# Attention and routed experts on one core: scores by half blocks in quarters of the array, probabilities turned by products with the unit matrix

## The chip, the cores and the metric

The kernel runs on one core of a Trainium2 chip. The metric is the device time in microseconds of one execution; 753.51 us is the median of three runs before the change.

## What is computed

The attention part works on 4 batches with 8 heads, 768 positions and 64 columns per head. Each query sees the 4 first keys (the sinks) and a window of 128 keys that ends with its own; its result is the row of the expert part, 3072 rows of 512 columns. Each row then goes to two of 8 experts (512 to 1024 to 512, with a rectifier between).

```python
keep = is_sink | in_window            # pos < 4, or 0 <= rel < 128
scores = np.where(keep, scale * q @ k.T, -1e9)
a = np.exp(scores - scores.max(-1)); a = a / (a.sum(-1) + 1e-9)
attn_out = a @ v
# experts
noisy = x @ w_gate + np.log1p(np.exp(x @ w_noise)) * noise
top2, top2_w = two largest of noisy, softmax over the two
out[mask] += top2_w[mask, k, None] * (np.maximum(x[mask] @ w1[e], 0) @ w2[e])
```

## The kernel before, in words

The program has two phases. The first is the attention of all batches, with the routing of a batch woven in behind it; the second is the experts. A batch has 4 pairs of heads; a pair, g, has its two heads in the two halves of the partitions. Each pair takes 3 steps, so there are 48 steps n, and a step works on two blocks of 128 queries for two heads, four units in all.

For a step, `qk` (L389) makes the scores of one block at a time, twice per step: a stationary tile of 128 queries against the block before and the block itself, 2 x 132 columns (4 of them sinks). The two heads use the upper and the lower half of the array's rows. Each of the two calls takes a buffer of two banks, S. `prev` (L392, ScalarE) moves the scores of the older block and the sinks, 132 columns for each unit, into `cbuf`; `cur` (L399, VectorE) puts the newer block's scores over those of the older block where the key is not later than the query. By that a unit keeps 132 columns, since exactly one of the keys j and j + 128 is in the window. In the first block of a pair `cur` is an addition of a mask (L397). `mins` (L409, VectorE) takes the maximum, `minus_max` (L412, GpSimd) negates it, `exps_sums` (L423, ScalarE) makes the exponentials with their sums.

`ptr` (L465, L468) turns the probabilities by transposes on TensorE into a buffer P of two banks; on odd steps also the sink columns that `pcopy` (L458, GpSimd) has laid together for two steps. `ptr_c` (L474, ScalarE) moves the turned tile to CT; `ptr_m` (L484, GpSimd's affine select) makes CM, the same with the older block's part set to zero. `pv` multiplies CT with the values of the older block (L494) and CM with `dv`, the difference of the two blocks' values (L497; the difference is L300, on GpSimd for two pairs in four, else on VectorE). `sinks` (L509) adds the sinks' part, `pv_c` (L517, ScalarE) moves the result, `rows` (L523, VectorE) turns it for the store. L436 (GpSimd) and L450 (VectorE) make the reciprocals of the sums.

S, P and the logits' buffer A share three double banks (`HELD = dict(D=3, X=2)`); X, the result of `pv`, has two single banks. Values and differences have two buffers each (`vn=2, dv=2`), so the values of a pair can be loaded when the pair two before it is done.

Every operation of the first phase is registered with its engine, and the order in which they are issued is the list `ORDER`, a list of operation numbers written out by hand; each engine then runs its instructions in that order, the SP queue its loads and stores as well. `replay` also gives each S, P, A and X its bank, by the time at which a planner expects a bank to be free. On SP, four writes of the routing weights (L848, `keep`) and the loads of keys (L364) and values (L367) stand in one queue. In the routing, L822 and L828 count rows by products with a matrix of ones, and the results of a batch give the first rows of expert 0.

The second phase is a list of matrix products, L1157 to L1159 (up, three products with split weights and rows) and L1223 to L1225 (down), ordered by the planner.

## Time and profile before

| | |
|---|---|
| median of 3 runs | 753.51 us (750.51 to 756.1) |
| profiled execution | 756.2 us, of which its span 754.6 us |
| mean granted clock of TensorE | 0.988 |
| busy in the span | PE 729.2, PEld 618.4, DVE 418.1, ACT 339.5, POOL 393.6 us |
| instructions | 13413 |

PE is TensorE's products, PEld its weight loads, DVE is VectorE, ACT ScalarE, POOL GpSimd. The times of two executions differ by some tenths of a per cent, so the profiled one is compared with its own span and not with the median.

### The profile page before, as it was taken

To read this page: it belongs to the slowest core of one execution; us is meant where nothing else is said; L and a number is where in the kernel's file an instruction comes from. 1 tells how busy PE (TensorE), PEld (TensorE's weight loads), DVE (VectorE), ACT (ScalarE), POOL (GpSimd) and SP (SyncE) were. 2 spreads that over 40 slices of the span, in tenths; PEclk is the share of its full clock that TensorE was granted. 3 is DMA by queue.
4 is the path that set the end of the run, shared out by engine and by line. 5 is a ranking of instruction groups with operands and counts; after the bars stand their busy time and mean duration, and the time that the engine had idled before them with its cause. 6 is when DMAs were issued, how large, how long until landed. Compare 5 with 4: busy or idle time off the path is not lost.

```text
span 754.6 us, 13413 instructions
## 1 busy us (share of the span) xinstructions
PE 729.2 (97%) x4787; PEld 618.4 (82%) x4787; DVE 418.1 (55%) x1082; ACT 339.5 (45%) x907; POOL 393.6 (52%) x640
## 2 busy tenths in 40 slices
PE   8999899889999999999999999999999999999995
PEld 4766666567889898889889988998899999999994
DVE  5779688786754654654365446535652664473420
ACT  5999799785224413341333243323432441343221
POOL 4346458771237385456636573747284755647212
PEclk9999899989999999999999999999999999999998
DMA  6557687945546743553445354526351653454033
GB/s 227 194 174 221 147 260 170 266 89 153 155 145 145 241 100 60 152 144 63 87 141 132 51 98 144 123 50 154 128 101 28 157 165 62 83 172 74 15 43 43
DMA packets 58310, 97.30 MB, mean 129 GB/s; under 512 B 19296, under 2 KB 31840, under 8 KB 58240
## 3 DMA queue, kind: packets, MB, share of 16 engines
q1 hardware_dynamic: 44864, 68.82, 30.3%
q0 software_dynamic: 13376, 27.60, 20.5%
q8 instruction: 38, 0.62, 0.4%
q14 instruction: 32, 0.26, 0.1%
HBM read 67.99 MB, written 28.40 MB: 128 GB/s over the span
## 4 chain that ended last, share of the span: by engine, by line
PE 77%; ACT 8%; issue 4%; DMA 4%; DVE 3%; POOL 2%; POOLq 0%; ACTq 0%; SPq 0%; DVEq 0%
PE H L1159 11%; PE H L1157 11%; PE H L1158 11%; PE Y L1224 11%; PE Y L1225 11%; PE Y L1223 11%; ACT cbuf L423 4%; PE D L389 3%; PE X L494 1%; ACT cbuf L392 1%; ACT CT L474 1%; PE Y L1228 1%; PE Y L1229 1%; POOL out L1247 1%; PE X L350 1%
## 5 line engine op out<-in xcount | busy, mean ns | idle before, releaser
L1008 POOL DMA_INDIRECT xg<-x_rows,rt_idq x174 | 174.2, 1001 | 60.9 <-issue 51.3
L1204 ACT ACTIVATE h<-H 128x384 fp32r<-128x384 f32 (+4 forms) x127 | 63.8, 503 | 254.5 <-PE H L1159 254.3
L1158 PE MATMUL H<-sqn,w 128*128 128x384 f32 (+4 forms) x508 | 174.0, 343 | 0.9 <-DVE sqn L300 0.9
L1157 PE MATMUL H<-skn,w 128*128 128x384 f32 (+4 forms) x508 | 174.5, 344 | 0.0
L1159 PE MATMUL H<-skn,w 128*128 128x384 f32 (+4 forms) x508 | 174.3, 343 | 0.0
L1212 DVE SCALAR_TENSOR_TENSOR h<-H,h 128x384 fp32r<-128x384 f32 (+4 forms) x167 | 75.1, 470 | 163.7 <-ACT h L1204 163.2
L1247 POOL DMA_INDIRECT out<-y,idx x53 | 93.7, 1767 | 50.5 <-ACT y L1232 34.9
L1256 POOL COPY spacer<-h 1x1 f32<-1x1 f32 x88 | 28.0, 319 | 147.4 <-ACT h L1204 147.2
L1158 PEld LDWEIGHTS H<-sqn,w 128*128 128x128 f32 x508 | 95.4, 188 | 7.7 <-DVE sqn L300 1.2
L1157 PEld LDWEIGHTS H<-skn,w 128*128 128x128 f32 x508 | 95.4, 188 | 7.4 <-ACT skn L1075 0.4
L1159 PEld LDWEIGHTS H<-skn,w 128*128 128x128 f32 x508 | 95.3, 188 | 2.1
L423 ACT ACTIVATE cbuf<-cbuf,nb 128x132 f32<-128x132 f32 x192 | 75.6, 412 | 2.4 <-POOL nb L412 2.4
L1225 PE MATMUL Y<-w2a,h 128*128 128x512 f32 x192 | 75.6, 394 | 0.0
L1225 PE MATMUL Y<-w2b,h 128*128 128x512 f32 x192 | 75.6, 394 | 0.0
L1224 PE MATMUL Y<-w2a,h 128*128 128x512 f32 x192 | 75.5, 393 | 0.0
L1224 PE MATMUL Y<-w2b,h 128*128 128x512 f32 x192 | 75.5, 393 | 0.0
L1223 PE MATMUL Y<-w2b,h 128*128 128x512 f32 x192 | 75.1, 391 | 0.0
L1223 PE MATMUL Y<-w2a,h 128*128 128x512 f32 x192 | 74.8, 389 | 0.0
L389 PE MATMUL D<-kq 64*128 64x264 f32 (+1 forms) x384 | 57.1, 406 | 9.2 <-DVE cbuf L399 3.6
L1075 ACT ACTIVATE skn<-xtn 128x512 fp32r<-128x512 f32 (+2 forms) x46 | 27.8, 605 | 58.5 <-DVE xtn L1066 58.4
L389 PEld LDWEIGHTS D<-kq 64*128 64x128 f32 x384 | 31.6, 192 | 21.1 <-DVE cbuf L399 6.0
L399 DVE COPY_PREDICATED cbuf<-le,D 128x256 f32<-128x256 uint8 x80 | 34.7, 445 | 18.4 <-ACT cbuf L392 17.8
(210 smaller groups left out, 1203.8 us busy)
## 6 DMA issues: line engine op xcount, KB each, us to landing
st<-in_w1l SPq DMA_DIRECT2D x32, 512.0 KB, 4.4
st<-in_w2l SPq DMA_DIRECT2D x32, 512.0 KB, 4.1
kq<-in_kq SPq DMA_DIRECT2D x15, 792.0 KB, 6.5
out<-zt SPq DMA_DIRECT2D x31, 256.0 KB, 5.6
vn<-in_v SPq DMA_DIRECT2D x16, 384.0 KB, 5.8
x_rows<-xr SPq DMA_DIRECT2D x48, 128.0 KB, 5.0
xg<-x_rows,rt_idq POOLq DMA_INDIRECT x174, 2.8
out<-y,idx POOLq DMA_INDIRECT x53, 5.1
```

Of the source, the lines that this page charges most:

```text
L389: nc.tensor.matmul(p[:, :2 if j else 1], kq(g)[r, j // 2, 2 + j % 2, NS:], x[:, :2 if j else 1], start=True, stop=True)
L423: nc.scalar.activation(C(n)[:, u], C(n)[:, u], AF.Exp, bias=get("nb", n)[:, u:u + 1], scale=1.0 / math.sqrt(D), accum_out=get("sm", n // 2 ...
L1008: nc.gpsimd.indirect_dma_start(out=x[:, i, :], out_offset=None, in_=xbuf.rearrange("r (q d) -> (r q) d", d=sh.SW), in_offset=bass.Indirect ...
L1157: nc.tensor.matmul(p, w[:, 0], xh, start=(i == 0), stop=False)
L1158: nc.tensor.matmul(p, w[:, 0], xl, start=False, stop=False)
L1159: nc.tensor.matmul(p, w[:, 1], xh, start=False, stop=(i == sh.DM // 128 - 1))
L1204: nc.scalar.activation(get("h", FC * q + f, [128, 2 * 128 * FIRST], F32R)[:, :width], H(q, f), AF.Relu)
L1212: nc.vector.scalar_tensor_tensor(h[:, o:o + s1 - s0], p[:, s0:s1], 0.0, h[:, s0:s1].bitcast(F32), op0=OP.max, op1=OP.subtract)
L1223: nc.tensor.matmul(p, hh, w[:, 0], start=(f == 0), stop=False)
L1224: nc.tensor.matmul(p, hh, w[:, 1], start=False, stop=False)
L1225: nc.tensor.matmul(p, hl, w[:, 0], start=False, stop=(f == FC - 1))
L1247: d = nc.gpsimd.indirect_dma_start(out=out, out_offset=bass.IndirectOffsetOnAxis(ap=c["idx"][:size(e, t), e, t:t + 1], axis=0), in_=get("y ...
```

## The change: what it does

The layout of the keys and queries in memory becomes one row of 6 blocks of 132 columns (128 keys and the 4 sinks) for the keys, and one for the queries. `qk` is called once per step. Each block of 128 queries is cut into two halves of 64; a half sees 196 columns in one piece, 128 keys from the start of its window, the sinks between, and 64 more. A product has 64 rows (a head) and 64 columns of queries (a half), so the four products of a block take the four quarters of the array. The four units of a step lie in one buffer of two banks. `prev` moves the first 132 columns of all units in one instruction, on ScalarE or VectorE; `cur` puts the last 64 columns over the first 64 in one instruction. In the first block of a pair, `cur0` adds a mask to the 132 columns before that, and `nosink` falls away.

`ptr` makes 16 products of 64 x 64 with the unit matrix in place of 8 transposes of 64 x 128 (20 in place of 10 on odd steps); `pcopy` takes two instructions, since the sinks lie in other columns in the two halves.

Some operations can now stand on another engine, as the string `SIDE` says for each: of 48 moves `prev`, 11 go to VectorE (6 of these on ordinary steps, 5 on first ones); of the 24 moves `ptr_c` of even steps, 7; of the 48 `pv_c`, 15; 11 of 48 `minus_max`, 7 of 24 `sums_e` and 3 of 16 `cur1` go from GpSimd to VectorE; 15 of 24 `pcopy` go from GpSimd to ScalarE. All 16 differences `dv` are on GpSimd, and a third of the `ptr_m` (16 of 48) on VectorE, where they read P. The order is another one, and `BANKS` names the banks.

```diff
@@ -18,7 +18,7 @@
-PR = dict(load_qk=0.0, load_v=24.264, w1=36, pc_pool=0, gap_8=1, dv_pool=2, et=42, cm_pool=12, gap=4, subs=0)
+PR = dict(load_qk=0.0, load_v=24.264, w1=36, pc_pool=0, gap_8=1, dv_pool=4, et=42, cm_pool=8, gap=4, subs=0)
@@ -38,54 +38,57 @@
 ORDER = """
...
+0 1 8 72 2 4 73 9 10 12 6 14 11 16 118 18 13 20 74 22 15 3 24 26 17 28 30 173 19 32 5 34 76 221 21 36 38 120 23 40
...
+"""
+SIDE = """
+11000011101001010001000100100000001000000011001000000100000100010100010000110000110000000100010000010000000010001111
+00010010111000001011010000011000101100100100010010100010100000001000010000100100000100010001011101011001000001001000
+"""
+BANKS = """
+00120120110120012001120101200112001012001012012001011001012102101020121102021120211102100121010021102011100210112112
+0110210020011001121002201201210102002010210100112012
@@ -124,10 +128,15 @@
-    def op(self, eng, dur, prio, fn, r=(), w=(), u=(), lat=None, kind=0):
+    def op(self, eng, dur, prio, fn, r=(), w=(), u=(), lat=None, kind=0, alt=None):
+        if alt:
+            self.alts.append((i, (eng, dur, kind), alt))
+            if SIDE.replace("\n", "")[len(self.alts) - 1:len(self.alts)] == "1":
+                eng, dur, kind = alt
+            fn.__defaults__ = fn.__defaults__[:-1] + (eng,)
@@ -240,12 +249,13 @@
-                    x = self.slot[kx] = len(r) - 1 if kx in last else min(range(len(r)), key=lambda x: r[x])
+                    x = self.slot[kx] = int(banks[len(self.slot)]) if banks else len(r) - 1 if kx in last else min(
+                        range(len(r)), key=lambda x: r[x])
@@ -303,13 +313,17 @@
-    m0 = consts.tile([128, 128], F32, name="m0")
-    nc.vector.tensor_scalar(m0, jp, 0.0, -BIG, op0=OP.is_gt, op1=OP.mult)
+    half = slice(0, 64), slice(64, 128)
+    m0 = consts.tile([128, KW], F32, name="m0")
+    nc.vector.memset(m0, -BIG)
+    for r, o, x in ((half[0], 0, jp[:, :128]), (half[1], 0, jp[:, 64:128]), (half[1], 64 + NS, jp[:, :64])):
+        nc.vector.tensor_scalar(m0[r, o:o + x.shape[1]], x[r], 0.0, -BIG, op0=OP.is_gt, op1=OP.mult)
-    nc.vector.tensor_copy(m1, m0[:, :NS])
-    nc.vector.memset(m0[:, :NS], 0.0)
-    le = consts.tile([128, 128], U8, name="le")
-    nc.vector.tensor_scalar(le, jp, 0.0, None, op0=OP.is_le)
+    nc.vector.tensor_scalar(m1, jp[:, :NS], 0.0, -BIG, op0=OP.is_gt, op1=OP.mult)
+    nc.vector.memset(m0[half[0], :NS], 0.0)
+    le = consts.tile([128, 64], U8, name="le")
+    for r in half:
+        nc.vector.tensor_scalar(le[r], jp[r, r], 0.0, None, op0=OP.is_le)
@@ -333,7 +347,7 @@
-    KW = 128 + NS
+    KW, BW = 128 + NS, 192 + NS
@@ -371,45 +385,58 @@
-    def keys(g, j0):
-        t = kq(g).rearrange("p g x k -> p (g x) k")
-        f = j0 // 2 * 4 + j0 % 2
-        return t[:, f:f + 2] if j0 % 2 == 0 else t[:, f:f + 4:3]
-
-    def qk(n, a):
-        g, j, _ = at(n, 2 * a)
-        for h in range(2):
-            r = slice(h * D, (h + 1) * D)
-            p = get("S", 2 * n + a, [128, 2, 512], F32, "ps")[:, h, :2 * KW].rearrange("p (a b) -> p a b", a=2)
-            x = keys(g, max(j - 1, 0))[r]
-            nc.tensor.matmul(p[:, :2 if j else 1], kq(g)[r, j // 2, 2 + j % 2, NS:], x[:, :2 if j else 1], start=True, stop=True)
-
-    def prev(n, a):
-        nc.scalar.activation(C(n)[:, 2 * a:2 * a + 2, :], get("S", 2 * n + a)[:, :, :KW], AF.Copy)
-
-    def cur(n, a):
-        c, p = C(n)[:, 2 * a:2 * a + 2, NS:], get("S", 2 * n + a)
-        if at(n, 2 * a)[1] == 0:
-            nc.vector.tensor_tensor(c, p[:, :, NS:KW], m0[:, None, :].to_broadcast([128, 2, 128]), op=OP.add)
+    def scores(n):
+        return get("S", n, [128, 2, 512], F32, "ps")[:, :, :2 * BW].rearrange("p h (a k) -> p a h k", a=2)
+
+    def qk(n):
+        for a in range(2):
+            g, j, _ = at(n, 2 * a)
+            for i in range(2):
+                for h in range(2):
+                    r, t = slice(h * D, (h + 1) * D), slice(64 * i, 64 * i + 64)
+                    k, x = kq(g)[r, 0].rearrange("p b k -> p (b k)"), scores(n)[t, a, h]
+                    k0 = KW * (j - 1) + 64 * i
+                    for o, f, w in ((0, k0, BW),) if j else ((0, 64 * i, KW - 64 * i), (64 + NS, 0, 64))[:1 + i]:
+                        nc.tensor.matmul(x[:, o:o + w], kq(g)[r, 1, j, t], k[:, f:f + w], start=True, stop=True)
+
+    def moved(eng, out, x):
+        if eng == "DVE":
+            nc.vector.tensor_copy(out, x)
-            nc.vector.copy_predicated(c, le[:, None, :].to_broadcast([128, 2, 128]), p[:, :, KW + NS:2 * KW])
-
-    def nosink(n):
-        nc.gpsimd.memset(C(n)[:, :2, :NS], -BIG)
-
-    def cur1(n):
-        c = C(n)[:, 2:, NS:2 * NS]
-        nc.gpsimd.tensor_tensor(c, c, m1[:, None, :].to_broadcast([128, 2, NS]), op=OP.add)
+            nc.scalar.activation(out, x, AF.Copy)
+
+    def small(eng):
+        return nc.gpsimd if eng == "Pool" else nc.vector
+
+    def old(n):
+        return int(n % NJ == 0)
+
+    def units(n):
+        return C(n).rearrange("p (a h) k -> p a h k", a=2)
+
+    def prev(n, eng):
+        moved(eng, units(n)[:, old(n):], scores(n)[:, old(n):, :, :KW])
+
+    def cur0(n):
+        nc.vector.tensor_tensor(units(n)[:, 0], scores(n)[:, 0, :, :KW], m0[:, None, :].to_broadcast([128, 2, KW]), op=OP.add)
+
+    def cur(n):
+        c = units(n)[:, old(n):, :, :64]
+        nc.vector.copy_predicated(c, le[:, None, None, :].to_broadcast([128, 2 - old(n), 2, 64]), scores(n)[:, old(n):, :, KW:])
+
+    def cur1(n, eng):
+        c = C(n)[:, 2:, :NS]
+        small(eng).tensor_tensor(c, c, m1[:, None, :].to_broadcast([128, 2, NS]), op=OP.add)
-    def minus_max(n):
-        nc.gpsimd.tensor_scalar(get("nb", n, [128, 4]), get("mn", n), -1.0 / math.sqrt(D), None, op0=OP.mult)
+    def minus_max(n, eng):
+        small(eng).tensor_scalar(get("nb", n, [128, 4]), get("mn", n), -1.0 / math.sqrt(D), None, op0=OP.mult)
@@ -432,8 +459,8 @@
-    def sums_e(m):
-        nc.gpsimd.tensor_scalar(get("sm", m), get("sm", m), 1e-9, None, op0=OP.add)
+    def sums_e(m, eng):
+        small(eng).tensor_scalar(get("sm", m), get("sm", m), 1e-9, None, op0=OP.add)
@@ -450,28 +477,30 @@
-        t = pcbuf[:, m % plan.rings["pc"]].rearrange("p (g x u s) -> p g x u s", g=2, x=4, u=4)[:, :, 0]
-        c = cbuf[:, 2 * (m % (plan.rings["C"] // 2)):][:, :2, :, :NS]
-        if eng == "ACT":
-            nc.scalar.activation(t, c, AF.Copy)
-        else:
-            (nc.gpsimd if eng == "Pool" else nc.vector).tensor_copy(t, c)
+        for i in range(2):
+            r, k = slice(64 * i, 64 * i + 64), 64 if i else 128
+            t = pcbuf[r, m % plan.rings["pc"]].rearrange("p (g x u s) -> p g x u s", g=2, x=4, u=4)[:, :, 0]
+            c = cbuf[r, 2 * (m % (plan.rings["C"] // 2)):][:, :2, :, k:k + NS]
+            if eng == "ACT":
+                nc.scalar.activation(t, c, AF.Copy)
+            else:
+                (nc.gpsimd if eng == "Pool" else nc.vector).tensor_copy(t, c)
-        for u in range(4):
-            for i in range(2):
-                r = slice(64 * i, 64 * i + 64)
-                nc.tensor.transpose(p[:, i, 64 * u:64 * u + 64], C(n)[r, u, NS:], idf[r, r])
-        for i in range(2 if n % 2 else 0):
-            r = slice(64 * i, 64 * i + 64)
-            nc.tensor.transpose(p[:, i, 256:320], pcbuf[r, n // 2 % plan.rings["pc"], :], idf[r, r])
+        for u in range(5 if n % 2 else 4):
+            for t in range(2):
+                for i in range(2):
+                    r = slice(64 * i, 64 * i + 64)
+                    x = C(n)[r, u] if u < 4 else pcbuf[r, n // 2 % plan.rings["pc"], :]
+                    k = (68 - 68 * t if i else 64 * t) if u < 4 else 64 * t
+                    nc.tensor.matmul(p[64 * t:64 * t + 64, i, 64 * u:64 * u + 64], x[:, k:k + 64], idf[r, r], start=True, stop=True)
-    def ptr_c(n):
-        nc.scalar.activation(get("CT", n, [128, 4, 128]).rearrange("p u (i s) -> p u i s", i=2), turned(n), AF.Copy)
+    def ptr_c(n, eng=0):
+        moved(eng, get("CT", n, [128, 4, 128]).rearrange("p u (i s) -> p u i s", i=2), turned(n))
@@ -513,8 +542,8 @@
-    def pv_c(n):
-        nc.scalar.activation(xt(n), get("X", XA[n])[:, :2, :], AF.Copy)
+    def pv_c(n, eng):
+        moved(eng, xt(n), get("X", XA[n])[:, :2, :])
@@ -563,24 +592,22 @@
+            need = {jj, max(jj - 1, 0)}
+            op("PE", .68 if jj else .61, n + P(g, "qk"), lambda n=n: qk(n), r=[("kq", g, i) for i in need], w=[("S", n)],
+               u=[("kq", g), ("C", n)], kind=3)
+            op("ACT", .46 if jj else .27, n + P(g, "prev"), lambda n=n, e=0: prev(n, e), r=[("S", n)], w=[("C", n, 0)], u=[("C", n)],
+               alt=("DVE", .61 if jj else .34, 0))
-                op("Pool", .05, n + P(g, "nosink"), lambda n=n: nosink(n), w=[("C", n, 0)], u=[("C", n)])
-            for a in range(2):
-                z = n + .2 * a
-                s = 2 * n + a
-                need = [jj] if not jj or a else [jj - 1, jj]
-                op("PE", .45 if jj or a else .26, z + P(g, "qk"), lambda n=n, a=a: qk(n, a),
-                   r=[("kq", g, i) for i in {jj, *need}], w=[("S", s)], u=[("kq", g), ("C", n)], kind=1)
-                if jj or a:
-                    op("ACT", .27, z + P(g, "prev"), lambda n=n, a=a: prev(n, a), r=[("S", s)], w=[("C", n, a)], u=[("C", n)])
-                op("DVE", .335, z + P(g, "cur"), lambda n=n, a=a: cur(n, a), r=[("S", s)], w=[("C", n, a)], u=[("C", n)])
+                op("DVE", .34, n + P(g, "cur"), lambda n=n: cur0(n), r=[("S", n)], w=[("C", n, 0)], u=[("C", n)])
+            op("DVE", .335 if jj else .2, n + P(g, "cur"), lambda n=n: cur(n), r=[("S", n)], w=[("C", n, 0)], u=[("C", n)])
-                op("Pool", .15, n + .4 + P(g, "cur1"), lambda n=n: cur1(n), w=[("C", n, 1)], u=[("C", n)])
-            op("DVE", .62, n + .4 + P(g, "mins"), lambda n=n: mins(n), r=[("C", n, 0), ("C", n, 1)], w=[("mn", n)], u=[("C", n)])
+                op("Pool", .15, n + .4 + P(g, "cur1"), lambda n=n, e=0: cur1(n, e), w=[("C", n, 0)], u=[("C", n)], alt=("DVE", .085, 1))
+            op("DVE", .62, n + .4 + P(g, "mins"), lambda n=n: mins(n), r=[("C", n, 0)], w=[("mn", n)], u=[("C", n)])
-                op("Pool", .15, n + .4 + P(g, "sub"), lambda n=n: minus_max(n), r=[("mn", n)], w=[("nb", n)])
+                op("Pool", .15, n + .4 + P(g, "sub"), lambda n=n, e=0: minus_max(n, e), r=[("mn", n)], w=[("nb", n)],
+                   alt=("DVE", .072, 1))
@@ -597,10 +624,12 @@
-                op(pe, {"Pool": .25, "ACT": .15, "DVE": .1}[pe], n + .5 + P(g, "pcopy"), lambda m=m, pe=pe: pcopy(m, pe), r=cs, w=[("pc", m)])
-            op("PE", .3 if odd else .24, n + .5 + P(g, "ptr"), lambda n=n: ptr(n), r=[("C", n)] + ([("pc", m)] if odd else []),
-               w=[("P", n)], kind=1)
-            op("ACT", .48, n + .5 + P(g, "ptr_c"), lambda n=n: ptr_c(n), r=[("P", n)], w=[("CT", n)])
+                op(pe, {"Pool": .45, "ACT": .3, "DVE": .2}[pe], n + .5 + P(g, "pcopy"), lambda m=m, e=0: pcopy(m, e), r=cs, w=[("pc", m)],
+                   alt=("ACT", .3, 0))
+            op("PE", .56 if odd else .45, n + .5 + P(g, "ptr"), lambda n=n: ptr(n), r=[("C", n)] + ([("pc", m)] if odd else []),
+               w=[("P", n)], kind=3)
+            op("ACT", .48, n + .5 + P(g, "ptr_c"), lambda n=n, e=0: ptr_c(n, e), r=[("P", n)], w=[("CT", n)],
+               alt=None if odd else ("DVE", .6, 0))
@@ -609,7 +638,8 @@
-                    op("Pool", .15, n + .6 + P(g, "sums_i"), lambda m=m: sums_e(m), r=[("sm", m, 0), ("sm", m, 1)], w=[("sm", m)])
+                    op("Pool", .15, n + .6 + P(g, "sums_i"), lambda m=m, e=0: sums_e(m, e), r=[("sm", m, 0), ("sm", m, 1)],
+                       w=[("sm", m)], alt=("DVE", .072, 1))
@@ -617,10 +647,11 @@
-                   w=[("X2", i) for i in xas], u=[("X", i) for i in xas], kind=4)
+                   w=[("X2", i) for i in xas], u=[("X", i) for i in xas], kind=5)
-                op("ACT", .27, n + .6 + P(gi, "pv_c"), lambda i=i: pv_c(i), r=[("X2", xi)], w=[("xt", i)], u=[("xtn", gi), ("X", xi)])
+                op("ACT", .27, n + .6 + P(gi, "pv_c"), lambda i=i, e=0: pv_c(i, e), r=[("X2", xi)], w=[("xt", i)],
+                   u=[("xtn", gi), ("X", xi)], alt=("DVE", .335, 0))
@@ -1526,14 +1557,10 @@
-    def turned(x):
-        x = x.reshape(B, HP, 2, NB // 2, 2, 128, D).transpose(0, 1, 2, 6, 3, 4, 5)
-        return x.reshape(B * HP, 128, NB // 2, 2, 128)
-
-    kt = turned(k)
-    kq = np.zeros((B * HP, 128, NB // 2, 4, NS + 128), np.float32)
-    kq[..., NS:] = np.concatenate([kt, turned(q)], axis=3)
-    kq[:, :, :, :2, :NS] = kt[:, :, :1, :1, :NS]
+    kq = np.zeros((B * HP, 128, 2, NB, 128 + NS), np.float32)
+    for i, x in enumerate((k, q)):
+        kq[:, :, i, :, :128] = x.reshape(B, HP, 2, NB, 128, D).transpose(0, 1, 2, 5, 3, 4).reshape(B * HP, 128, NB, 128)
+    kq[:, :, 0, :, 128:] = kq[:, :, 0, :1, :NS]
```

## Rows read from the trace of the kernel before

**Rows 1.** Busy time by stretch: us, PE, PEld, DVE, ACT, POOL busy (instructions), PEclk, DMA share, GB/s.
```profile
13.30:178.70 165.40, 150.90 (x1899) 108.78 (x1898) 125.00 (x376) 146.94 (x595) 94.97 (x242) 0.96 0.67 185
13.30:82.00 68.70, 64.46 (x818) 46.59 (x817) 52.13 (x150) 67.17 (x288) 34.57 (x100) 1.00 0.64 183
82.00:178.70 96.70, 86.45 (x1081) 62.20 (x1081) 72.87 (x227) 79.77 (x307) 60.41 (x142) 0.93 0.69 187
...
220.00:720.00 500.00, 499.10 (x2478) 447.05 (x2477) 254.46 (x581) 170.98 (x268) 276.57 (x352) 1.00 0.46 109
```

**Rows 2.** Waits of TensorE from 178 to 300 us: total us, times, longest.
```profile
PE H L1158 <- DVE sqn L300: 0.9, 1, 0.9
```

**Rows 3.** Chain that ended last, shares by line: first from 13.3 to 82, then to 178.7 us.
```profile
by line: ACT cbuf L423 32.1%; DMA vn<-in_v 8.9%; ACT cbuf L392 8.5%; ACT CT L474 8.0%; PE D L389 8.0%; issue 7.2%; PE X L494 5.0%; PE X L497 2.9%; PE D L465 2.6%; ACT xtn L517 2.5%; POOL dv L300 2.3%; ACT ps L501 2.0%; PE X L509 1.9%; POOL 
...
by line: PE D L389 11.5%; ACT cbuf L423 9.5%; PE X L494 7.6%; DMA xg<-x_rows,idg 6.4%; DMA x_rows<-rt_w 5.9%; issue 5.2%; PE X L497 5.1%; PE X L509 4.7%; PE D L465 4.4%; DVE cbuf L399 3.9%; ACT cbuf L392 3.6%; PE D L708 3.1%; ACT CT L474 3.
```

**Rows 4.** Instructions of TensorE in order of time: start us, us from first start to last end.
```profile
100.64 0.71 PE L389 MATMUL D<-kq 64*128 64x264 f32 x4 [0.44 <-ACT CT L474]
...
103.32 0.46 PE L465 MATMUL D<-idf,cbuf 64*128 64x64 f32 x8
...
103.62 1.11 PE L389 MATMUL D<-kq 64*128 64x264 f32 x8
...
106.72 0.71 PE L465 MATMUL D<-idf,cbuf 64*128 64x64 f32 x16
...
111.33 0.45 PE L828 MATMUL D<-m,one 128*128 128x56 bf16 x12
...
189.62 0.76 PE L828 MATMUL X<-m,one 128*128 128x56 bf16 x24
```

**Rows 5.** Pieces of the chain that ended last: start us, us, what.
```profile
17.34 0.55 ACT cbuf L392 x2
...
19.43 0.48 ACT CT L474
...
62.25 0.27 ACT xtn L517
...
75.60 6.11 DMA vn<-in_v
```

**Rows 6.** Groups by line and shape, 13.3 to 178.7 us: count, busy us, mean ns, idle before.
```profile
L399 DVE COPY_PREDICATED cbuf<-le,D 128x256 f32<-128x256 uint8 x75 | 32.4, 444 | 16.4 <-ACT cbuf L392 15.8
...
L409 DVE TENSOR_REDUCE mn<-cbuf 128x4 f32<-128x528 f32 x46 | 31.7, 692 | 2.1 <-POOL cbuf L406 1.8
...
L300 POOL TENSOR_TENSOR dv<-vn 128x640 f32<-128x640 f32 x7 | 10.8, 1548 | 2.1 <-DMA vn<-in_v 2.1
...
L300 DVE TENSOR_TENSOR dv<-vn 128x640 f32<-128x640 f32 x8 | 6.5, 812 | 2.8 <-DMA vn<-in_v 2.8
...
L458 POOL COPY pcbuf<-cbuf 128x32 f32<-128x32 f32 x24 | 5.3, 221 | 8.0 <-ACT cbuf L423 7.9
```

**Rows 7.** Waits from 20 to 179 us, TensorE and its weight loads: total, times, longest.
```profile
PE D L389 <- DVE cbuf L399: 3.6, 6, 2.0
...
PEld D L389 <- DVE cbuf L399: 5.5, 10, 2.2
```

**Rows 8.** VectorE and SP in order of time, 66 to 84 us.
```profile
71.02 4.48 SPq L848 DMA_DIRECT2D x_rows<-rt_w  x4
...
81.73 0.83 DVE L300 TENSOR_TENSOR dv<-vn 128x640 f32<-128x640 f32 x1 [2.49 <-DMA vn<-in_v]
```

**Rows 9.** Busy time by stretch, as in the first group, where the granted clock fell.
```profile
84.70:91.50 6.80, 6.80 (x60) 5.00 (x54) 4.16 (x12) 5.20 (x22) 3.04 (x8) 0.50 0.11 42
156.40:163.20 6.80, 6.30 (x46) 4.45 (x44) 5.02 (x18) 5.61 (x23) 4.52 (x16) 0.50 0.38 24
```

21 lines of the change are left out of this document (11 added, 10 removed), and 90 rows, old and new, of the table ORDER.

## The prediction

> **What bounds the kernel now.** I read the busy time by stage first, then the waits, then the chain that ended last. From 178.7 us on TensorE never stops for long: it is busy 499.1 of the 500 us from 220 to 720 [rows 1], and the only wait of TensorE from 178 to 300 us is 0.9 us [rows 2]. The expert phase is therefore a solid block, and the change does not touch it. What the change can do is move the moment at which that block begins. So the sum is made on the attention phase alone, and each microsecond there counts once.
>
> The attention phase has two parts. Until 82 us ScalarE is busy 67.2 of 68.7 us [rows 1], 98%; the chain of waits there is led by L423, the exponentials, with 32%, then L392 and L474, all ScalarE [rows 3]. By the order list that part covers about steps 0 to 24 of 48. After 82 us ScalarE has 79.8 of 96.7 us and nobody leads: L389 11.5%, L423 9.5%, two transfers 12% [rows 3]. TensorE shows 150.9 of 165.4 us busy over the whole phase, but its records carry their start and drain: eight transposes alone take 0.46 us, sixteen in a run 0.71 us [rows 4], so eight more cost 0.25 us and 0.21 us are paid once per run. ScalarE has no slack in the first part; TensorE, with 64.46 of 68.7 us [rows 1], has 4.2.
>
> **Scores.** A half step (264 columns, both heads beside each other) costs 1.11 - 0.71 = 0.40 us [rows 4]. Before, an ordinary step has two, 0.80 us. After, each half step is four products of 196 columns in the four quarters, 0.40 x 196/264 = 0.30 us if all four run at once: 0.59 us a step, -0.21 us. The first step of a pair goes from 0.60 to 0.50 us. 32 x 0.21 + 16 x 0.10 = -8.2 us of TensorE.
>
> **Turning the probabilities.** Eight transposes (ten on odd steps) at 0.25/8 = 31 ns become 32 records (16 products of two records each, 40 on odd steps) of 64 columns. No row shows four quarters at work. Lower bound: the score rate, 0.40/2 per record of 264 columns, so 49 ns for a round of four, 8 rounds 0.39 us. Upper bound of the same idea: the round takes what a pair of transposes takes, 62 ns, 0.50 us. I take 56 ns, between the two: 0.45 and 0.56 us against 0.25 and 0.31. 24 x 0.20 + 24 x 0.25 = +10.8 us (+7.7 to +13.6). Counted in the two order lists, TensorE changes its split of the array 156 times before and 146 times after; at 0.21 us [rows 4] that is -2.1 us. TensorE in all: -8.2 + 10.8 - 2.1 = +0.5 us (-2.6 to +3.3). It is even, so the gain has to come from elsewhere.
>
> **ScalarE.** Two moves of the kept half cost 0.55 us in the chain, one move of a turned step (512 elements) 0.48 us [rows 5]. The new single move has 528 elements: 0.50 us, between 0.48 and 0.55. On ordinary steps 32 x 0.55 becomes 26 x 0.50 (six go to VectorE): -4.6 us; on first steps five of 16 at 0.27 us leave: -1.4 us. Seven turned copies leave at 0.48 us, -3.4 us, and 15 result copies at 0.27 us [rows 5], -4.1 us. Fifteen copies of the sink probabilities arrive, two small instructions each: at most 0.54 us (two of the 0.27 us kind), at least 0.2; I take 0.3, as 32 elements lie nearest the small end: +4.5 us (+3.0 to +8.1). Sum -9.0 us (-5.4 to -10.5). Sorted by step, about -4.7 us fall into steps 0 to 23, where ScalarE sets the pace, and -4.3 us into the rest.
>
> **VectorE.** The merge was 80 instructions at 0.444 us [rows 6]. Now there are 32 of that size and 16 of half of it (0.28 us, an estimate by size): 35.5 to 18.7, -16.8 us. Eight differences of the values leave for GpSimd: 8 x 0.812 [rows 6] = -6.5 us. Arrivals are priced at the 692 ns of a 528-element reduction [rows 6], 1.31 ns per element: kept halves 6 x 0.69 + 5 x 0.35, turned copies 7 x 0.67, result copies 15 x 0.34, masked copies (16 leave GpSimd) 12 x 0.67 + 4 x 0.34, and 21 tiny ones at no more than the 0.22 us of the sink copy [rows 6]: 5.9 + 4.7 + 5.1 + 9.4 + 4.6 = 29.7 us. Net +6.4 us: from 125.0 to 131 of 165 us [rows 1]. Still not the bound, but less able to catch up.
>
> **GpSimd.** +8 x 1.548 us for the differences [rows 6], -12 x 0.67 - 4 x 0.34 for the masked copies, about -6 us for sink copies and tiny ones that leave: +12.4 - 9.4 - 6 = -3 us of 95.0.
>
> **Score buffers.** A step took two of the three double banks for scores and one for turning; it now takes one and one. TensorE waited 3.6 us, its weight loads 5.5 us, for a merge to release such a bank [rows 7]; these are the same stalls seen twice. I put at most 3.6 us here, and count none, since the next thing is late then as well (the maximum of the step before). The new layout of the keys moves the same bytes, and the loads of pair 0 lie under the warm-up: nothing, up to a few tenths at the start if that cover is gone.
>
> **The new order and its queues.** At 81.73 us VectorE had stood 2.49 us for the values of one pair [rows 8]. The load was issued at 75.60 us and took 6.11 us [rows 5]. On the SP queue it stood behind the four writes of L848, which began at 71.02 us and took 4.48 us [rows 8]. VectorE, blocked in its queue, held up the merges of the following step; ScalarE then waited for scores, and right behind, from 84.7 to 91.5 us, the granted clock was 0.50 [rows 9], which is 1.2 GHz. In the new list this load stands ahead of the four writes, and VectorE has no differences any more. But the wait does not vanish. GpSimd now holds all 16 differences; behind the one in question stand the negated maximum of step 21 and the routing weights, for which the four writes wait; behind these on SP waits the values' load of the next pair, and behind its difference on GpSimd the maximum of step 25. I credit 2 us of the 2.49 us and of what follows it, no more.
>
> **The sum.** In the first part ScalarE frees 4.7 us, but TensorE is late next: it has 4.2 us of slack there and loses none of its work, and two engines that feed each other don't both come to 100%, so I count half: -2.3 us. In the second part ScalarE is busy 82%; half of its 4.3 us: -2.1 us. The stall: -2 us. TensorE +0.5 us. VectorE's +6.4 us lie mostly in its idle fifth; I charge an eighth, +0.8 us. Together -5.1 us (with ScalarE and the stall in full -9.0 - 2.5 + 0.5 = -11; with half of ScalarE's low end, the stall kept and TensorE's upper end -2.7 + 3.3 + 0.8 = +1.4). The profiled execution took 756.2 us with a span of 754.6; the median of the three runs is 753.5, so the profiled one stands 2.7 us above it. From 756.2 that gives 751.1 us for an execution like it, and 748.4, say 748 us, for the median.
>
> **Rivals.**
> *The stalls and the low clock go (mechanism of the order).* Two stretches of 6.8 us ran at half the clock, the second from 156.4 to 163.2 us. Each loses up to 3.4 us. For it: the first follows TensorE's longest wait for a merge, 2.0 us [rows 7]. Against: routing, loads and weight splits still share the four queues. It gives another 6.8 us, and the rest of the stalls some 1 us: 741 us. The Trainium skill, "TensorE: Matmul & The Clock Gate", Part 4, says that the full clock doesn't engage in transpose mode, which doesn't count as TensorE work in the same way; products in place of transposes would then help to the same 741 us. The trace does not bear this out much: the clock was 1.00 from 13.3 to 82 us [rows 1] with eight to ten transposes in each step.
> *Nothing comes of it.* ScalarE's time is given back, as TensorE costs its upper +3.3 us, VectorE's added 6.4 us lie ahead of merges, and the values' loads hold up GpSimd's maxima. Speaks for it: TensorE and ScalarE are both above 90% until 82 us [rows 1]. Then the first three terms of the sum shrink to some -2 us in all and the last two stay: -0.7 us, 753 us.
> *Slower: the quarters are not fed fast enough.* The densest train of small products in the trace is L828: twelve records take 0.45 us and 24 take 0.76 us [rows 4], 26 ns each, and no row sustains a closer pitch. If 26 ns holds between records over all quarters, 32 records cost 0.83 us and 40 cost 1.04: +24 x 0.58 + 24 x 0.73 = +31.4 us instead of +10.8, TensorE +21 us. TensorE would then have 150.9 + 21 = 172 us of work in the phase; were it as full as ScalarE is in the first part, 98%, the phase would take 175.5 us in place of 165.4: +10 us, 764 us. It decides from the point at which this full TensorE alone takes the 165.4 us, 11 us more than now, which is a round of four of 80 ns. Against it: pairs start side by side, so that eight transposes come at 31 ns each although each runs far longer. Should quarters run only in pairs, the scores cost 1.19 us a step and the turning 0.8 to 1.0: over +40 us; I give this almost nothing. The Trainium skill, same page, section "Wait — 56ns, not 53.3ns?", puts the floor from start to start at about 25 ns however small the product; by it the time would be the 764 us. Part 3 of the page has concurrent tiles start some 4 ns apart, by which it would be the 748 us. The trace agrees with the first for one tile and cannot tell for four.
>
> **How the numbers follow.** This kernel's measurement tells about 1% from no change, 746.0 to 761.0 us. Forecast 0.45 (own range 743 to 752, a third of it below 746), stalls gone 0.20 (735 to 744), nothing 0.20 (751 to 756), slower 0.15 (757 to 775, a fifth of it below 761). Faster 0.15 + 0.20 = 0.35, slower 0.12, the rest 0.53. The range leaves out about a tenth at each end: 737 to 761 us.
>
> **What would show it.** Scores: a step's 16 score records in about 0.6 us plus one drain. Turning: 32 records in about 0.45 us plus a drain; 0.8 us would be the slow rival. ScalarE's busy time before the first expert product about 9 us lower, VectorE's about 6 higher. The first product of the experts at about 174 us in place of 178.7. No half clock near 85 us. The prediction is wrong if TensorE's queue is filled with drains of the new split, or if GpSimd's wait for the values appears in front of each negated maximum.

## The result, and the profile after

The changed kernel took 759.53 us (median of 19 runs, 753.34 to 764.59) against 753.51 us (19 runs, 748.88 to 759.18): a ratio of 1.0064 (the two means are 758.5 and 753.7 us), 95% interval 1.0043 to 1.0084. On another chip, later, it was 753.93 against 750.67 us, 1.0038 (1.0017 to 1.0060). The change costs some 3 to 5 us. The time lies inside the forecast range, and within the 1% that the forecast called no change, but the sign is wrong: the forecast was 5 us faster.

The profiled execution took 754.74 us with a span of 753.1. Its busy time by stretch answers to [rows 1], the line at 0.50 of the clock to [rows 9]; the last line ends at the experts' first product:
```profile
13.30:178.70 165.40, 146.44 (x3564) 112.79 (x3560) 128.61 (x401) 140.28 (x559) 84.81 (x193) 0.98 0.69 186
13.30:82.00 68.70, 64.72 (x1640) 50.23 (x1640) 51.93 (x157) 63.05 (x259) 31.32 (x76) 1.00 0.69 191
82.00:178.70 96.70, 81.72 (x1930) 62.56 (x1926) 76.68 (x245) 77.23 (x301) 53.48 (x118) 0.96 0.69 183
220.00:720.00 500.00, 500.00 (x2485) 448.52 (x2484) 256.18 (x582) 172.21 (x270) 277.75 (x354) 1.00 0.47 109
...
117.50:124.30 6.80, 5.97 (x108) 4.83 (x110) 5.87 (x17) 5.15 (x23) 2.44 (x10) 0.50 0.90 177
...
13.30:178.84 165.54, 146.57 (x3565) 112.93 (x3562) 128.75 (x401) 140.28 (x559) 84.81 (x193) 0.98 0.69 186
```
The expert phase is the same solid block. ScalarE lost 6.7 us of busy time before it, VectorE gained 3.6, GpSimd lost 10.2, TensorE shows 4.5 less, and yet the experts' first product starts at 178.84 us, where it started at 178.72 before. The profile of before had two stretches at 0.50 of the clock [rows 9], this one has one, so on equal terms the attention phase became longer. In the last line TensorE is busy 146.57 of 165.54 us: 19.0 us of waiting, against 14.5 in [rows 1]. On the later chip the changed kernel's profile has 18.2 us of it:
```profile
13.30:177.63 164.33, 146.09 (x3560) 113.17 (x3553) 128.92 (x399) 139.60 (x556) 84.67 (x192) 0.98 0.67 187
```

The chain that ended last, shares by line from 13.3 to 82 and from 82 to 178.7 us, answers to [rows 3]:
```profile
by line: PE D L497 15.0%; ACT cbuf L450 13.1%; PE D L404 9.8%; PE X L523 8.1%; ACT cbuf L410 5.6%; ACT CT L410 5.6%; PE X L526 5.4%; PE X L364 4.7%; PE X L538 4.7%; issue 4.1%; DVE mn L436 3.8%; ACT xtn L410 3.4%; DVE cbuf L429 2.9%; DVE CM
...
by line: ACT cbuf L450 21.2%; issue 7.2%; PE D L497 6.3%; ACT CT L410 6.0%; DMA out<-zt 5.5%; PE X L523 5.2%; ACT cbuf L410 4.5%; PE X L526 3.4%; DMA x_rows<-xr 3.0%; POOL w L310 2.9%; DVE mn L436 2.8%; DVE xr L552 2.8%; PE X L538 2.7%; PE 
```
In the first part the exponentials (L450, L423 before) fall from 32% to 13%, and TensorE's turning (L497) leads with 15%.

TensorE in order of time, where [rows 4] had the transposes and half steps:
```profile
95.15 0.69 PE L497 MATMUL D<-idf,cbuf 64*64 64x64 f32 x32
...
96.42 0.69 PE L497 MATMUL D<-idf,cbuf 64*64 64x64 f32 x32
96.93 0.30 PE L497 MATMUL D<-idf,pcbuf 64*64 64x64 f32 x8
...
107.54 0.89 PE L404 MATMUL D<-kq 64*64 64x196 f32 x16
```
The 32 records of a turned step take 0.69 us from first start to last end, where eight transposes took 0.46 [rows 4]; with the eight of the sinks it is 0.81 (96.42 to 97.23). So eight records more cost 0.12 us, 60 ns a round of four, and the 32 of one step take 0.51 us to the start of the next run (96.42 to 96.93), 64 ns a round: near the 56 ns taken, and far from the 80 ns from which the slower rival decides.

Groups by line and shape, as in [rows 6]:
```profile
L410 ACT ACTIVATE cbuf<-D 128x528 f32<-128x528 f32 x25 | 14.9, 606 | 2.2 <-PE D L404 2.1
L429 DVE COPY_PREDICATED cbuf<-le,D 128x256 f32<-128x256 uint8 x30 | 13.4, 452 | 4.7 <-ACT cbuf L410 4.4
...
L485 ACT ACTIVATE pcbuf<-cbuf 64x32 f32<-64x32 f32 x30 | 6.9, 230 | 0.4
...
L487 POOL COPY pcbuf<-cbuf 64x32 f32<-64x32 f32 x18 | 3.7, 207 | 6.3 <-ACT cbuf L450 5.6
```
The merge of a step costs 0.45 us, as taken. On ScalarE the last number is the length of one record, and records overlap: the next one starts before the last has ended. What an instruction takes of the queue is the time from its start to the next one's:
```profile
163.38 0.59 ACT L410 ACTIVATE cbuf<-D 128x528 f32<-128x528 f32 x1
163.87 0.46 ACT L485 ACTIVATE pcbuf<-cbuf 64x32 f32<-64x32 f32 x2
164.35 0.60 ACT L410 ACTIVATE CT<-D 128x512 f32<-128x512 f32 x1
```
The single move takes 0.49 us like this, as taken (0.50). A pair of sink copies takes 0.48 here and some 0.50 as a rule, where 0.30 was taken.

### The profile page after: what moved, and what is told of

It reads as the page before. It is cut to its first block, busy times and chain, and to the rows that moved or that the text cites. A ratio compares the mean times of both kernels' runs of the same rounds, so it can differ in the third digit from the quotient of the medians.

```text
span 753.1 us, 16796 instructions
## 1 busy us (share of the span) xinstructions
PE 723.6 (96%) x6531; PEld 622.6 (83%) x6531; DVE 426.3 (57%) x1116; ACT 333.6 (44%) x872; POOL 384.3 (51%) x589
## 4 chain that ended last, share of the span: by engine, by line
PE 79%; ACT 8%; issue 4%; DVE 4%; DMA 2%; POOL 2%; SPq 0%; POOLq 0%; DVEq 0%; ACTq 0%
PE H L1190 12%; PE H L1188 12%; PE H L1189 12%; PE Y L1255 11%; PE Y L1256 11%; PE Y L1254 11%; ACT cbuf L450 4%; PE D L497 2%; PE D L404 1%; PE X L523 1%; ACT CT L410 1%; PE Y L1259 1%; PE Y L1260 1%; ACT cbuf L410 1%; POOL out L1278 1%
## 5 line engine op out<-in xcount | busy, mean ns | idle before, releaser
L450 ACT ACTIVATE cbuf<-cbuf,nb 128x132 f32<-128x132 f32 x192 | 75.2, 398 | 9.7 <-POOL nb L439 7.3
L404 PE MATMUL D<-kq 64*64 64x196 f32 (+3 forms) x832 | 39.7, 317 | 3.2 <-DMA kq<-in_kq 1.5
L1176 DVE TENSOR_TENSOR gw<-xg,perm 32x8 f32<-32x8 f32 x174 | 27.3, 157 | 27.2 <-DMA xg<-x_rows,rt_idq 23.6
L1256 PEld LDWEIGHTS Y<-w2b,h 128*128 128x128 f32 x192 | 36.0, 188 | 7.8
```

The source lines that it names most:

```text
L404: nc.tensor.matmul(x[:, o:o + w], kq(g)[r, 1, j, t], k[:, f:f + w], start=True, stop=True)
L450: nc.scalar.activation(C(n)[:, u], C(n)[:, u], AF.Exp, bias=get("nb", n)[:, u:u + 1], scale=1.0 / math.sqrt(D), accum_out=get("sm", n // 2 ...
L1256: nc.tensor.matmul(p, hl, w[:, 0], start=False, stop=(f == FC - 1))
```

## The experiments

All ratios are to the kernel before on the same chip, with 95% intervals.

**Which part of the change.** Theory W was that the new work itself costs TensorE more than it frees; theory O, that the loss lies in the new order and in the engines to which work moved. Four kernels undo one or several of these.

*The moves undone:*
```
-SIDE = """ 1100001110100101...          +SIDE = """ 0000000000000000...
```


> The changed kernel with none of the 69 moves between engines (every operation of the string SIDE on its first engine); order, banks, differences on GpSimd and a third of the masked copies on VectorE stay. Theory O (the loss lies in the order and the moves, which put waits in front of the negated maxima and merges): ratio to before 1.000 to 1.010, not clearly better than the changed kernel's 1.0064, since the order was written for the moves. Theory W (the new work itself costs TensorE more than it frees elsewhere): 1.006 to 1.015, as ScalarE gets back about 13 us of work.

Measured: 769.04 us, 1.0233 (1.0217 to 1.0249). *The moves undone, and GpSimd's share of differences and masked copies as before:*
```
-dv_pool=4, cm_pool=8, SIDE as above     +dv_pool=2, cm_pool=12, SIDE all zeros
```


> As the one before, and also the differences of values back on VectorE for two pairs in four and all masked copies back on GpSimd (five of them placed later in the list, behind the copy they then read). So the new work and the new order on the old engines. O: about 1.00 to 1.01. W: 1.006 to 1.015.

Measured: 770.81 us, 1.0261 (1.0243 to 1.0279). *The old order too, each whole step standing where its second half step stood:*
```
-ORDER = the new list                    +ORDER = the list of before, renumbered, banks given anew; SIDE all zeros, dv_pool=2, cm_pool=12
```


> The new work (scores in quarters, one merge, turning by products) on the old engines and in the old order: each new operation stands where the last of the operations stood that it replaces; the banks are named again for it. O: the new work by itself is at least as good as before, ratio 0.990 to 1.000. W: slower than before by as much as the changed kernel or more, 1.005 to 1.015.

Measured: 763.82 us, 1.0175 (1.0141 to 1.0208). *Only the differences of the values back where they were:*
```
-dv_pool=4                               +dv_pool=2
```


> The changed kernel with the differences of values back on VectorE for two pairs in four, all else as changed. O, in the form that GpSimd's waits for the values hold up the negated maxima: 0.998 to 1.004. If that queue is not the cause: 1.005 to 1.009 as the changed kernel.

Measured: 756.16 us, 1.0059 (1.0045 to 1.0074), the changed kernel's own ratio: where the differences are made is not the cause. The first three read as "the new work costs 1.75%, and the moves and the new order win most of it back", so theory O seemed to fall. That reading did not last either: the last two runs show that these three numbers contain a wait of another kind.

**One part alone.** Theory T: the products that turn the probabilities cost TensorE's time, which sets the pace. Theory L: the longer chain of a step costs. *The kernel before, with products in place of transposes:*
```
-  nc.tensor.transpose(p[:, i, 64*u:64*u+64], C(n)[r, u, NS:], idf[r, r])
+  for t in (slice(0, 64), slice(64, 128)):
+      nc.tensor.matmul(p[t, i, 64*u:64*u+64], C(n)[r, u, NS:][:, t], idf[r, r], start=True, stop=True)
...                                                                # the sinks likewise
```


> One part of the change alone: the kernel before, in its own order, with its own scores, moves and merges, but the probabilities turned by 64x64 products with the unit matrix, two where one transposition stood (32 and 40 records a step, +10.8 us of TensorE by the prediction's price). Theory T (the products are what costs): TensorE had 4.2 us of slack until 82 us and nobody led after it, so most of the 10.8 us comes through: ratio 1.008 to 1.015, 758 to 763 us. Theory L (what costs is the longer chain of a step: all 16 scores, then one move, then one merge of all four units): no more than 3 us: ratio 1.000 to 1.004.

Measured: 759.46 us (758.71 to 760.24) against 749.91, 1.0118 (1.0088 to 1.0148). Theory T. Here the products of 64x64 stand between scores of 64x128, as neither the kernel before nor the changed one has it; TensorE in order of time:
```profile
105.25 0.69 PE L466 MATMUL D<-idf,cbuf 64*64 64x64 f32 x32
105.87 1.16 PE L389 MATMUL D<-kq 64*128 64x264 f32 x8
```
The 32 records take 0.62 us to the start of the scores, beside 0.51 to a run of their own split in the changed kernel: the change of split costs 0.11 us.

*The changed kernel, the lower half turned by transposes again:*
```
+  nc.tensor.transpose(p[:, 0, 64*u:64*u+64], C(n)[:64, u, :128], idf[:64, :64])
-  for t in range(2): for i in range(2): matmul(...)
+  for t in range(2): for i in range(1, 2): matmul(...)
```


> The changed kernel, with the 64 queries of the lower half turned by one transposition a unit again, as before, and only the upper half by two products: 24 and 30 records a step instead of 32 and 40, about -5.4 us of TensorE over the phase at 14 ns a record; the same order and the same outputs. Theory T: 3 to 5 us come back against the changed kernel: ratio to the kernel before 0.999 to 1.003. Theory L: nothing comes back: 1.004 to 1.008.

Measured: 863.44 us, 1.1481 (1.1430 to 1.1533); both theories missed it by 100 us. TensorE in order of time and by stretch, in an execution of 877.68 us:
```profile
62.18 0.48 PE L499 MATMUL D<-idf,cbuf 64*64 64x64 f32 x4
62.59 0.37 PE L493 MATMUL D<-idf,cbuf 64*128 64x64 f32 x1
62.88 0.48 PE L499 MATMUL D<-idf,cbuf 64*64 64x64 f32 x4
```
```profile
13.30:82.00 68.70, 68.70 (x693) 48.96 (x689) 24.24 (x66) 32.94 (x125) 15.41 (x36) 0.67 0.30 92
61.90:65.40 3.50, 3.50 (x29) 2.33 (x25) 0.01 (x1) 0.74 (x4) 0.00 (x0) 0.50 0.00 0
```
One unit of five records takes 0.70 us from start to start here, at half the clock, where 32 records took 0.51 from the start of one run to that of the next at the full one. Each unit changes the array's split twice, between 64x128 and 64x64. From the last record ahead of a change to the first one behind it 0.29 and 0.24 us pass in the stretches at half the clock (medians, into 64x64 and out of it), 0.20 and 0.15 us at the full one. The run says nothing on theories T and L.

*The changed kernel, with half of the products issued twice to the same place:*
```
+  for _ in range(2 if u < 2 else 1):
       nc.tensor.matmul(p[64*t:64*t+64, i, 64*u:64*u+64], x[:, k:k+64], idf[r, r], start=True, stop=True)
```


> The changed kernel, with the products of units 0 and 1 issued twice, to the same place (16 more records a step, 0.23 us at 14 ns each, +11 us of TensorE over 48 steps). Theory T: TensorE is what is late in the phase, so 7 to 11 us come through: ratio to the kernel before 1.015 to 1.021. Theory L: the waits within a step take most of it up: 1.007 to 1.011.

Measured: 773.69 us, 1.0318 (1.0281 to 1.0354): theory T, and more than its upper end.

*The changed kernel, move and merge in two instructions again:*
```
-  moved(eng, units(n)[:, old(n):], scores(n)[:, old(n):, :, :KW])
+  for a in range(old(n), 2):
+      moved(eng, units(n)[:, a], scores(n)[:, a, :, :KW])        # the merge likewise
```


> The changed kernel, with the move and the merge of a step each cut in two again (one instruction for each block of 128 queries), so that the first can begin after 8 of 16 score records; by the rows of before a half move costs 0.28 and a half merge 0.45 us, so ScalarE or VectorE works 0.1 to 0.25 us longer a step. Theory L: the chain of a step is 0.5 to 0.9 us shorter and the time falls under the changed kernel: ratio to the kernel before 0.998 to 1.003. Theory T: the added work of ScalarE and VectorE shows or nothing does: 1.005 to 1.012.

Measured: 755.64 us, 1.0075 (1.0046 to 1.0104). Nothing comes back; theory L in this form falls.

**What a microsecond is worth on the other engines.** Theory S: the engines take turns, so that added work shows wherever it is put.
```
+  nc.vector.tensor_copy(extra, ge)                                  # behind the row maxima, or
+  nc.scalar.activation(extra[:, :32], ge[:, :32], AF.Copy)          # behind the exponentials
```


> The changed kernel with one more copy on VectorE a step, of 128 columns of a constant to a tile that nobody reads, behind the row maxima: some 0.2 us each by the rows of its other copies, +10 us of VectorE over 48 steps, and no wait for anyone but through the queue. Theory T (TensorE alone sets the pace of the attention phase, so the products' time came through and the rest is cover): no more than 3 us come through, ratio 1.006 to 1.010. Theory S (the step is a chain in which the engines take turns and nobody has slack, so the 6.4 us that the change adds to VectorE cost nearly what they measure): 6 to 10 us, ratio 1.014 to 1.020.

> The changed kernel with one more copy of 32 columns on ScalarE a step, behind the exponentials, about 0.22 us each by the small copies of the turned sinks, +10.6 us of ScalarE over 48 steps. ScalarE was relieved of some 7 to 9 us by the change. Theory T: it has that slack now, so no more than 3 us come through, ratio 1.006 to 1.010. Theory S: 6 to 10 us, ratio 1.014 to 1.020.

> The kernel before with the same added copy of 128 columns on VectorE a step (+10 us of VectorE). Theory T: VectorE has slack, no more than 3 us: ratio 1.000 to 1.004. Theory S: 6 to 10 us: 1.008 to 1.013.

> The kernel before with the same added copy of 32 columns on ScalarE a step (+10.6 us of ScalarE). The prediction held ScalarE to be the bound until 82 us, so that half of what it is relieved of there would come back: by that 4.7 us are added where it leads, ratio 1.005 to 1.008. Theory T: TensorE leads and nothing much comes through, 1.000 to 1.004. Theory S: 8 to 10 us, 1.010 to 1.014.

Measured: 1.0102 (1.0076 to 1.0128), 1.0092 (1.0067 to 1.0117), 1.0037 (1.0014 to 1.0060) and 1.0029 (1.0005 to 1.0052). What was added, in the four traces in this order:
```profile
L438 DVE COPY extra<-ge 128x128 f32<-128x128 f32 x45 | 14.7, 326 | 0.0
```
```profile
L453 ACT ACTIVATE extra<-ge 128x32 f32<-128x32 f32 x46 | 10.2, 221 | 0.0
```
```profile
L411 DVE COPY extra<-ge 128x128 f32<-128x128 f32 x46 | 14.4, 312 | 0.0
```
```profile
L426 ACT ACTIVATE extra<-ge 128x32 f32<-128x32 f32 x46 | 11.1, 242 | 0.0
```
ScalarE in order of time, in the last of them:
```profile
44.21 0.32 ACT L426 ACTIVATE extra<-ge 128x32 f32<-128x32 f32 x1
44.33 0.48 ACT L393 ACTIVATE cbuf<-D 128x264 f32<-128x264 f32 x1
```
An added copy takes 0.12 us of ScalarE's queue, not the 0.24 us of its record, so the 48 of them added 5.8 us and not the 10.6 expected. In the kernel before, 14.4 us on VectorE cost 2.8 us of time, 0.2 us for each (0.1 to 0.3 by the interval), and 5.8 us on ScalarE cost 2.2, 0.4 for each (0.1 to 0.7). In the changed kernel, taken from its 1.0038 to 1.0064 on other chips, they cost 3 to 5 and 2 to 4 us. Theory S falls in the kernel before; in the changed one the answers lie at the upper end of theory T. Whether ScalarE sets the pace of the first part is not settled by this: half of what was added there came through, as the prediction had counted. From the exponentials of step 4 to those of step 24 the trace before has 57.4 us, the one with the added copies, 2.4 us of them in that stretch, 58.6.

**Single places of the order.** In the changed profile TensorE stood 3.2 us in three waits between 113.2 and 118.3 us, behind four subtractions of GpSimd (2.79 us from 109.58) that held up two negated maxima, and 2.0 us for masked copies that hold a bank for the gate's products. Theory P: TensorE's added waits are such places. Theory N: other waits take over.
```
-ORDER ... 1175 ... 1176 ... 1177 ... 1178 ... 763 ... 784 ... 794     +... 763 ... 725 1175 ... 784 1176 ... 794 1177 ... 829 1178
-cm_pool=8                                                             +cm_pool=12, eight masked copies behind the copies they read
```


> The changed kernel itself, on the same chip as the next three, to compare them with: 1.004 to 1.008 of the kernel before.

> The changed kernel with four entries of the order moved: GpSimd's four subtractions of a weight (2.79 us together, which stand ahead of the negated maxima of steps 32 and 33 in its queue, ScalarE, VectorE and TensorE waiting at 111 to 118 us) go behind them, one at a time. Theory P (the added idle time of TensorE is fixed in places of the order): the three waits of TensorE there, 3.2 us in the profile, shrink and 2 to 3 us come back: 0.002 to 0.004 less than the changed kernel on this chip. Theory N (the waits follow from the new work, and another wait takes over): within 0.0015 of the changed kernel.

> The changed kernel with all masked copies on GpSimd again, as before: 16 more on GpSimd, out of the copied probabilities, instead of on VectorE out of the bank, whose release the gate's products wait for twice (2.0 us in the profile) and a turning once (0.9 us). Eight of them had to go behind the copy that they now read. Theory P: 2 to 3 us come back (0.002 to 0.004 less than the changed kernel); GpSimd's 16 us more are hidden. Theory N: within 0.0015, or slower by what GpSimd's queue now delays.

> Both of the last two edits. Theory P: they add up, 4 to 6 us, and the time is that of the kernel before: 0.999 to 1.003. Theory N: 1.004 to 1.008.

Measured: 1.0038 (1.0017 to 1.0060), 1.0053 (1.0030 to 1.0075), 1.0075 (1.0043 to 1.0106) and 1.0048 (1.0024 to 1.0071). Nothing came back. With the subtractions moved the three waits are one of 1.5 us, and TensorE stands 2.46 us in one piece 20 us later, for the same releaser; its waits from 105 to 140 us:
```profile
PE D L497 <- DVE cbuf L429: 4.0, 2, 2.5
```
It was 2.1 us in the same stretch of the changed kernel. Theory N.

**The size of the piece.** Theory G: the whole step as one piece is what makes TensorE wait. *The new work by half steps, in the order and on the engines of before:*
```
-  op("PE", ..., lambda n=n: qk(n), ..., w=[("S", n)])           # 16 records, one bank
+  for a in range(2): op("PE", ..., lambda n=n, a=a: qk(n, a), ..., w=[("S", 2 * n + a)])   # prev and cur likewise
   ORDER, SIDE, dv_pool, cm_pool: as before
```


> The new work at the old size of piece: scores in quarters of 196 columns and turning by products as in the changed kernel, but scores, move and merge again by half steps, each half with a score bank of its own, and the order and the engines of the kernel before (its dv, masked copies and small operations where they stood). Beside the run with the products alone (1.0118) it has only the scores' quarters and the narrower merges more. Theory G (the whole-step piece makes TensorE wait: a bank is held over 16 records, a move and a merge, and nothing of the step can start before): TensorE's saving on the scores, 8 us or more, comes through: 0.999 to 1.004. Theory N (TensorE's waits come with the new work in any order that was not made for it, as in the run with whole steps in the old order, 1.0175): 1.010 to 1.018.

Measured: 766.22 us, 1.0221 (1.0189 to 1.0253). Neither theory had it; the waits of TensorE to 190 us and GpSimd in order of time show why:
```profile
PE D L502 <- POOL pcbuf L492: 6.8, 2, 4.5
```
```profile
132.03 1.24 POOL L1041 DMA_INDIRECT xg<-x_rows,idg  x1 [0.76 <-issue]
133.28 0.22 POOL L492 COPY pcbuf<-cbuf 64x32 f32<-64x32 f32 x1
138.85 0.21 POOL L492 COPY pcbuf<-cbuf 64x32 f32<-64x32 f32 x1 [5.35 <-DMA xg<-x_rows,idg]
```
The change makes the copy of the sink probabilities two instructions, one for each half. On GpSimd, behind a gather, the second of them stood until the gather had landed, 5.35 us, and the turning on TensorE stood with it. The trace has the reason in the program: this second copy waits for the semaphore (111) that this gather raises when it lands, and for the first copy; the first one waits for the exponentials alone. In one instruction, in the run with the products alone, the same copy stands in the same place, carries no wait for the gather and runs at once:
```profile
136.56 1.24 POOL L1004 DMA_INDIRECT xg<-x_rows,idg  x1 [0.76 <-issue]
137.81 0.22 POOL L458 COPY pcbuf<-cbuf 128x32 f32<-128x32 f32 x1
137.99 0.73 POOL L300 TENSOR_TENSOR w<-st,w 128x256 fp32r<-128x256 f32 x1
```
The runs with whole steps on the old engines have the same wait; GpSimd's waits in the old order:
```profile
POOL pcbuf L487 <- DMA xg<-x_rows,idg: 9.1, 3, 4.3
```
*The last kernel, with the three pairs behind a gather on ScalarE:*
```
+  pe = "ACT" if m in (18, 19, 23) else pe          # of the 24 sink copies
```


> The last kernel with three of the 24 pairs of sink copies (those right behind a gather on GpSimd) on ScalarE, nothing else changed. Theory Q (the copy in two instructions behind a gather is what costs in the old order): TensorE's 6.8 us of waiting for it go, 5 to 7 us come back: 0.007 to 0.009 less than the half steps' 1.0221, so 1.012 to 1.015. Theory N (waits move on to the next place, as they did when the four subtractions were moved): 1.018 or more.

Measured: 755.06 us (753.58 to 757.55), 1.0050 (1.0028 to 1.0073): theory Q, with 11 us (from 766.22 us, on another chip) instead of 5 to 7. Three pairs of 0.2 us copies that wait for a gather cost more than all the products, 8.8 us in the run with these alone. With the wait also the low clock went: 0.985 to 0.991 in the runs before this edit, 0.992 to 0.998 after it.

## Why the prediction was wrong

The step that failed is the one from freed work to a shorter phase. The sum held TensorE's own work even (+0.5 us) and let half of what ScalarE gets rid of (-2.3 and -2.1 us) and the stall (-2 us) come off the phase, so off TensorE's waits. TensorE's work did stay even, but its waits grew to 19.0 us, from 14.4 in the trace of the kernel before that has the full clock throughout (the one with the added ScalarE copies, first of the three below). That the time lies inside the stated range is luck: the upper edge of that range was drawn by the slower rival, whose mechanism did not come about.

Three of these traces have the full clock (1.00) over the whole attention phase, and so can be set side by side. Each row ends at the experts' first product; first the kernel before with the added ScalarE copies, then the products alone, then the new work by half steps with the three pairs moved:
```profile
13.30:173.83 160.53, 146.12 (x1889) 104.33 (x1889) 124.90 (x374) 148.67 (x636) 94.23 (x240) 1.00 0.67 189
```
```profile
13.30:182.27 168.97, 160.74 (x3171) 116.85 (x3167) 125.81 (x374) 149.40 (x591) 95.33 (x242) 1.00 0.65 182
```
```profile
13.30:178.89 165.59, 150.10 (x3582) 111.60 (x3577) 118.88 (x375) 148.45 (x600) 99.18 (x260) 1.00 0.66 187
```
TensorE's busy time goes from 146.1 to 160.7 with the products, and back to 150.1 with the quarters; its waits (length less busy) are 14.4, 8.2 and 15.5 us; the phase ends at 173.8, 182.3 and 178.9.

- *Turning and scores, sized about right.* Counted from each record's start to the next one's, or to its own end where TensorE waits, turning takes 19.5 us in the first of these traces and 31.4 in the last: +11.9 us, predicted +10.8 (+7.7 to +13.6). The scores take 46.6 and 37.9: -8.7 us, predicted -8.2.
- *Split changes.* The 14.6 us of the products alone are more than turning costs, since TensorE changes its split 200 times there, beside 152 and 154 times in the other two traces. The prediction's 0.21 us a change was read off transposes behind transposes [rows 4], which change nothing; in the run with products alone a change costs 0.11 us, about half of that.
- *TensorE in all.* Predicted +0.5 us. By half steps in the old order it is +4.0, and there the time went up by 3.7 us (755.06 against 751.33). By whole steps in the new order, as changed, it is at most 146.6 us beside 146.1, hence about even, as predicted.
- *The phase, the step that failed.* The stall at 81.73 us, credited with 2 us, did go (GpSimd, which makes all differences now, waits 1.2 us in all for values). But TensorE waits 4.6 us longer than in the kernel before at the full clock, in 28 waits of which the longest is 1.5 us; a second profile of the changed kernel has 18.2 us of waiting in all. Which of the three new things makes these waits, the whole-step piece, the order or the engines, was not separated. Together they gained nothing over half steps in the old order (1.0038 to 1.0064 against 1.0050). Of the 69 moves between engines, the traces show what one kind is good for: with them nine of the 24 pairs of sink copies stay on GpSimd, all before 100.1 us and so ahead of the first gather. The 1.0233 without them contains that wait (5.4 us of GpSimd); how much else they bring was not separated.
- *ScalarE.* Predicted -9.0 us, measured -6.7 (in the profile). The mis-sized term is the sink copies, 0.50 us a pair instead of 0.30, 3 us for 15 pairs. Credited with half, 4.4 us in the sum; at the 0.4 that the added copies cost in the kernel before, 6.7 us are worth 2.7 (0.4 to 4.5). So the half is not refuted, but in the changed kernel nothing of it is seen. *VectorE:* +3.6 instead of +6.4 us, at 0.2 worth 0.7, about what was charged. *GpSimd:* -10.2 instead of -3 us, which has no term in the sum.
- *The sum* with these prices would still be 2 us faster for the changed kernel (TensorE even, -2.7 and +0.7). It is 3 to 5 us slower, and the 5 to 7 us between are about the 4.6 us of added waits. By half steps the prices come nearer: +4.0 us on TensorE, of which 0.6 came through with the products alone, so +2.4 to +4.0, ScalarE about as before (148.5 us against 146.9 [rows 1]), and 6.0 us less on VectorE, -1.2: 1.2 to 2.8 us slower, against 3.7 measured there (2.1 to 5.5).
- *Rivals.* The one on the low clock did not come about: the changed kernel's runs on the first chip have a mean granted clock of 0.984 to 0.994, no higher than those of before on other chips (0.984 to 0.998). The slower one is refuted by the 60 ns a round. The Trainium skill ("TensorE: Matmul & The Clock Gate", "Wait — 56ns, not 53.3ns?") has a floor of about 25 ns from start to start; over four tiles the trace shows 15 ns a record, so it does not hold across tiles. "Nothing comes of it" has the right outcome (753 us, about what the later chip shows), not the reasons: TensorE did not cost its upper +3.3 us, and GpSimd waited for values once.

What stays open: why the products issued twice cost 19 to 21 us of time (the phase ends at 194.6 instead of 178.8 us) for about 13 us of work, and what makes TensorE's many small waits in the changed kernel. Splitting the move, moving four subtractions and giving GpSimd its masked copies did not find it.

No version here beats the kernel before. By half steps the products cost TensorE 11.9 us and the quarters give back 8.7; what they take off VectorE does not make up for that.
